# Seven products in place of eight for gate and value, their weights streamed from memory, and PReLU by two ScalarE passes throughout

## The chip, the cores and the metric

One core of a Trainium2 chip runs the whole kernel as one program. The metric is device time in microseconds (us). Its engines are TensorE (PE in the profile; PEld is its weight load), VectorE (DVE), ScalarE (ACT), GpSimd (POOL) and SyncE (SP), which issues all DMAs here. Each engine works through its own list of instructions in order. A scheduler has fixed those lists when the kernel was built, so that they can be read without running it.

## The reference

Three layers follow one another. The attention has 8 batches, 8 heads, 576 tokens and head size 64, and goes through 32 packed tokens; its output is a matrix `x` of 4608 tokens by 512. Then come two feed-forward layers:

```python
p_packed = sm_attn(p, k, v)
out = sm_attn(q, p_packed, p_packed)          # -> x, 4608 x 512
h = x @ w_in                                  # 512 x 2048
g = np.maximum(h, 0.0) + alpha * np.minimum(h, 0.0)
x = g @ w_out                                 # 2048 x 512
g = x @ w_gate                                # 512 x 1536
silu = g * (1.0 / (1.0 + np.exp(-g)))
val = x @ w_val                               # 512 x 1536
return silu * val @ w_out2                    # 1536 x 512
```

## The kernel before

Weights arrive as the bits of float64 numbers. `convert` turns a piece of 128 by 512 of them into float32 on the chip: one ScalarE, five VectorE and one GpSimd operation, and two more that split it into a high and a low part. A product of float32 accuracy is made of three TensorE passes over such parts (`mm3`, lines 281 to 283: low weight by high input, high by high, high by low).

**First layer.** An iteration (256 in all) takes 128 of the 2048 hidden numbers and 288 tokens. `h_unit` makes their hidden values `h` in a PSUM bank (tag `h`, two banks): six matmuls of 288 columns. PReLU follows, in iterations below `RELU` by two ScalarE rectifications and one VectorE operation (lines 699 to 701), from there on by two VectorE operations (lines 705 and 708). `split` then makes the high part on ScalarE (line 716) and the low part on GpSimd (line 718). `o_unit` multiplies them by `w_out` two iterations later (`LAG1`): 12 matmuls of 288 columns into the four banks `acc`. Beside these products run the attention of the next batch (`quad`), and `pp_win`, which multiplies its packed values by `w_in`.

**Second layer.** An iteration (108 in all) takes 128 hidden numbers and a block of `T` = 512 tokens. `gv_unit` makes `gps` (gate, tag `h`) and then `vps` (value, tag `at`), 12 matmuls of 512 columns each. ScalarE takes the sigmoid of `gps` (line 817), VectorE multiplies by `gps` and by `vps` (lines 818, 819), and `split` makes two parts. `out_unit` multiplies them by `w_out2` one iteration later (`LAG2`), 12 matmuls of 512 columns into `acc`. All weights of the layer lie in SBUF; their 36 pieces are converted by the table `PIECES2` in the last 40 iterations of the first layer and the first 6 of the second. The layer's input is read back from memory (`x1d`) and split block by block.

The order of the work around the change is set by tables of iterations (`plan`, `at`) and then by the scheduler, which moves instructions on each engine by what it expects to be ready.

Of the kernel before, what the change touches and what calls it, by code (L numbers as in the profile page):

```python
# [12 lines left out]
ALU = mybir.AluOpType  # L13
# [50 lines left out]
# The first layer's pieces in order: 128 columns of w_in, 128 rows of w_out.  # L64
# [10 lines left out]
# Later batches' attention: steps by iteration, for each group of four heads from its own start.  # L75
# [7 lines left out]
# Iterations from the second feed-forward's start: its weights' pieces, and load and split of its  # L83
# input, of the first block and of the next ones (from the start of the block before).
PIECES2 = {
    -40: 1, -35: 1, -32: 3, -31: 1, -24: 1, -23: 1, -7: 1, -3: 5, -2: 1, -1: 3, 1: 1, 2: 2, 4: 1,
    5: 3, 6: 7,
}
FIRST_X = ((-10, -8), (-6, -6), (-6, -4), (-1, -1))
NEXT_X = ((7, 11), (4, 5), (9, 9), (11, 11))  # L90

# High words of float64 numbers at the ends of float32's exponent range, as float32 bits.
# [9 lines left out]
def tile_kernel(  # L102
# [34 lines left out]
    NBLK = NT // T  # L137
# [25 lines left out]
    # ---- weights: float64 bits to float32, or to two float32r parts  # L163
    win, wout, wg, wv, wo2 = {}, {}, {}, {}, {}

    SLOTS = dict(wi="AABB", wo="AABB", wg="AAB", wv="BAB", wp="CCD")
# [37 lines left out]

    def convert(n=1):
        """The next n pieces of 128 by 512 numbers."""
        for src, parts in queue[:n]:
# [4 lines left out]
            issued.append(nc.sync.dma_start(out=like(raw, src), in_=src))  # L212
            words = raw.rearrange("p (n t) -> p n t", t=2)
            low, high = words[:, :, 0], words[:, :, 1]
            held = n_piece in HOLD
            with tc.issue_after(begun[HOLD[n_piece]].ins) if held else ExitStack():
                nc.scalar.activation(out=f32(val), in_=f32(high), func=AF.Abs)
            nc.vector.tensor_scalar(
                out=f32(val), in0=f32(val), scalar1=E_TOP, scalar2=E_LOW, op0=ALU.min, op1=ALU.max
            )  # L220
            nc.vector.tensor_scalar(
                out=val,
                in0=val,
                scalar1=3,
                scalar2=0x3FFFFFF8,
                op0=ALU.logical_shift_left,
                op1=ALU.bitwise_and,
            )
            nc.vector.scalar_tensor_tensor(
                out=val,  # L230
                in0=high,
                scalar=0xC0000000,
                in1=val,
                op0=ALU.bitwise_and,
                op1=ALU.bitwise_or,
            )
            nc.vector.tensor_scalar(
                out=high, in0=val, scalar1=0xFF800000, scalar2=None, op0=ALU.bitwise_and
            )
            dst = parts()  # L240
            light = len(dst) == 1
            if n_piece in BY_POOL:
                nc.scalar.activation(out=f32(low), in_=low, func=AF.Copy, scale=2.0**-52)
                nc.gpsimd.tensor_tensor(out=f32(low), in0=f32(low), in1=f32(high), op=ALU.mult)
            else:
                nc.vector.scalar_tensor_tensor(
                    out=f32(low),
                    in0=low,
                    scalar=2.0**-52,
                    in1=f32(high),  # L250
# [656 lines left out]
```

## Time and profile before

| | us |
|---|---|
| median of 3 runs | 1799.95 (1799.92 to 1800.79) |
| span of the profiled execution | 1797.2 |
| PE busy | 1712.5 (95% of the span) |
| DVE, ACT, POOL busy | 886.2, 534.1, 556.5 |
| first matmul of the second layer's gate | 883.55 |

The profile cuts the span into 40 slices; a digit is the busy share of a slice in tenths, and PEclk is the granted TensorE clock, in tenths of full speed:

```profile
PE   6698899999999999998788999999999999999999
DVE  7999965655656474778996312122121212121211
ACT  5765442323233332433332212111121212121111
POOL 3666622222222222366765211111111111111111
PEclk7899999999999999999999999999999999999999
```

The first five slices hold the attention of the first batches and the first layer's weights. Then the first layer runs; slices 17 to 22 hold the conversion of the second layer's weights, and the rest is the second layer.

### The profile page before, as it was taken

Reading aid. Unit: us, or ns where it says so; the run is one execution under the profiler, and the core shown is the slowest. Engines: PE = TensorE matmul, PEld = TensorE weight load, DVE = VectorE, ACT = ScalarE, POOL = GpSimd, SP = SyncE. Lnnn points to the kernel's source line nnn. Section 1 sums busy time; section 2 is a strip of 40 time slices with the busy share of each in tenths; the row PEclk is TensorE's granted clock in tenths of the full one; section 3 lists DMA queues with packets and bytes.
Section 4 is the critical chain, followed back from the end, with each engine's and each line's share of the span. In section 5 each row is a group of like instructions: output and inputs, shape, how many; then the busy total and the mean of one; then the engine's idle time right before and its main releaser. Section 6 shows DMA issues by size and latency. Waiting matters only on the chain.

```text
span 1797.2 us, 24797 instructions
## 1 busy us (share of the span) xinstructions
PE 1712.5 (95%) x9616; PEld 1433.5 (80%) x9616; DVE 886.2 (49%) x1509; ACT 534.1 (30%) x1125; POOL 556.5 (31%) x524
## 2 busy tenths in 40 slices
PE   6698899999999999998788999999999999999999
PEld 3477688888888888888666888888888888888887
DVE  7999965655656474778996312122121212121211
ACT  5765442323233332433332212111121212121111
POOL 3666622222222222366765211111111111111111
PEclk7899999999999999999999999999999999999999
DMA  9333451412222222113241101000010101010000
GB/s 241 109 103 122 132 129 42 81 27 55 43 52 53 55 53 42 61 40 107 93 132 50 56 1 47 1 30 18 1 47 1 47 1 47 1 36 1 24 0 24
DMA packets 179349, 99.13 MB, mean 55 GB/s; under 512 B 125984, under 2 KB 164896, under 8 KB 179232
## 3 DMA queue, kind: packets, MB, share of 16 engines
q1 hardware_dynamic: 179232, 97.56, 20.2%
q8 instruction: 75, 1.23, 0.3%
q14 instruction: 42, 0.34, 0.1%
HBM read 76.29 MB, written 21.23 MB: 54 GB/s over the span
## 4 chain that ended last, share of the span: by engine, by line
PE 78%; DVE 11%; issue 3%; ACT 2%; POOL 2%; DMA 2%; SPq 0%; POOLq 0%; DVEq 0%; ACTq 0%
PE acc L281 6%; PE acc L283 6%; PE acc L282 6%; PE o L281 5%; PE o L282 5%; PE vps L281 5%; PE vps L282 5%; PE o L283 5%; PE vps L283 5%; PE gps L283 5%; PE gps L282 5%; PE gps L281 5%; PE ppw L577 3%; PE h L281 3%; PE h L283 3%
## 5 line engine op out<-in xcount | busy, mean ns | idle before, releaser
L718 POOL TENSOR_TENSOR lo<-g,hi 128x288 fp32r<-128x288 f32 x256 | 220.8, 864 | 451.1 <-ACT hi L716 421.1
L718 POOL TENSOR_TENSOR lo<-s,hi 128x512 fp32r<-128x512 f32 x108 | 141.4, 1309 | 679.2 <-ACT hi L716 679.2
L818 DVE TENSOR_TENSOR s<-gps,s 128x512 f32<-128x512 f32 x108 | 74.6, 691 | 481.9 <-ACT s L817 481.9
L716 ACT ACTIVATE hi<-g 128x288 fp32r<-128x288 f32 x256 | 113.1, 443 | 357.8 <-DVE g L708 281.5
L705 DVE TENSOR_SCALAR g<-h,al 128x288 f32<-128x288 f32 x208 | 106.9, 514 | 171.6 <-PE h L283 154.1
L281 PE MATMUL h<-a2h,ppw 128*128 128x288 f32 x512 | 158.3, 309 | 18.2 <-DVE g L708 12.4
L817 ACT ACTIVATE s<-gps 128x512 f32<-128x512 f32 x108 | 64.4, 596 | 367.8 <-PE gps L283 367.8
L282 PE MATMUL h<-a2h,ppw 128*128 128x288 f32 x512 | 151.9, 297 | 0.0
L283 PE MATMUL h<-a2l,ppw 128*128 128x288 f32 x512 | 151.7, 297 | 0.0
L716 ACT ACTIVATE hi<-s 128x512 fp32r<-128x512 f32 x108 | 68.1, 631 | 254.8 <-DVE s L819 254.8
L819 DVE TENSOR_TENSOR s<-vps,s 128x512 f32<-128x512 f32 x108 | 74.5, 690 | 120.0 <-PE vps L283 119.8
L281 PEld LDWEIGHTS h<-a2h,ppw 128*128 128x128 f32 x512 | 96.7, 189 | 46.3 <-DVE g L708 18.3
L283 PEld LDWEIGHTS h<-a2l,ppw 128*128 128x128 f32 x512 | 96.3, 188 | 1.7 <-issue 1.7
L282 PEld LDWEIGHTS h<-a2h,ppw 128*128 128x128 f32 x512 | 96.9, 189 | 0.1
L708 DVE SCALAR_TENSOR_TENSOR g<-h,g 128x288 f32<-128x288 f32 x208 | 93.9, 453 | 4.4
L577 PE MATMUL ppw<-wi,ppT 128*64 128x512 f32 x256 | 78.0, 632 | 10.3 <-POOL wi L255 7.0
L281 PE MATMUL acc<-hi,wo0l 128*128 128x288 f32 x256 | 78.2, 310 | 4.5 <-ACT hi L716 3.7
L281 PE MATMUL acc<-hi,wo1l 128*128 128x288 f32 x256 | 74.8, 301 | 3.9 <-ACT hi L716 3.7
L282 PE MATMUL acc<-hi,wo0h 128*128 128x288 f32 x256 | 75.5, 300 | 0.0
L282 PE MATMUL acc<-hi,wo2h 128*128 128x288 f32 x256 | 75.3, 299 | 0.0
L281 PE MATMUL acc<-hi,wo2l 128*128 128x288 f32 x256 | 75.0, 299 | 0.1
L281 PE MATMUL acc<-hi,wo3l 128*128 128x288 f32 x256 | 74.6, 298 | 0.4 <-ACT hi L716 0.4
(224 smaller groups left out, 4556.8 us busy)
## 6 DMA issues: line engine op xcount, KB each, us to landing
cva<-in_moe_w_out_dram SPq DMA_DIRECT2D x24, 512.0 KB, 3.5
v<-in_v_dram SPq DMA_DIRECT2D x16, 576.0 KB, 4.8
out_dram<-os SPq DMA_DIRECT2D x36, 256.0 KB, 2.1
cva<-in_moe_w_in_dram SPq DMA_DIRECT2D x16, 512.0 KB, 3.6
kr<-in_k_dram SPq DMA_DIRECT2D x96, 72.0 KB, 2.7
qr<-in_q_dram SPq DMA_DIRECT2D x96, 72.0 KB, 2.4
x1d<-x1s SPq DMA_DIRECT2D x24, 288.0 KB, 2.1
cva<-in_moe_w_gate_dram SPq DMA_DIRECT2D x12, 512.0 KB, 3.7
```

The lines of the kernel that those rows point to most:

```text
L281: nc.tensor.matmul(o, wlo, xhi, start=start, stop=False)
L282: nc.tensor.matmul(o, whi, xhi, start=False, stop=False)
L283: nc.tensor.matmul(o, whi, xlo, start=False, stop=stop)
L577: nc.tensor.matmul(o[r, :], ppT[NQ * b + q2][:, r], w[:, 2 * q2 + pr, :], start=True, stop=True)
L705: nc.vector.tensor_scalar(out=g32, in0=hp, scalar1=0.0, scalar2=al[:, f : f + 1], op0=ALU.min, op1=ALU.mult)
L708: nc.vector.scalar_tensor_tensor(out=g32, in0=hp, scalar=0.0, in1=g32, op0=ALU.max, op1=ALU.add)
L716: nc.scalar.activation(out=hi, in_=x, func=AF.Copy)
L718: nc.gpsimd.tensor_tensor(out=lo, in0=x, in1=f32(hi), op=ALU.subtract)
L817: nc.scalar.activation(out=s, in_=pt["g"], func=AF.Sigmoid)
L818: nc.vector.tensor_tensor(out=s, in0=pt["g"], in1=s, op=ALU.mult)
L819: nc.vector.tensor_tensor(out=s, in0=pt["v"], in1=s, op=ALU.mult)
```

## The change

**Second layer, products.** Two blocks of 384 tokens (`T` = 384) form a super-block. Its input is cut into four parts by token block and by halves of the 512 inputs (A11, A12, A21, A22), and 128 columns of gate and of value into four likewise. Eight products of such parts would make gate and value for both blocks; seven products of sums and differences of parts do (Winograd's form of Strassen's scheme). `gv_step` runs one step, 72 in all: seven products of 6 matmuls of 384 columns, in three accumulations. `xb` (tag `h`) collects products 0 and 2, `yb` (tag `at`) products 1, 3 and 5, and `vb` (tag `h` again) products 4 and 6. The intermediate sums are read out of a bank in between, before the next product is added to it: `p1` by ScalarE, `u2`, `u3` and again `p1` by VectorE. Two blocks mean two results of 384 columns, one finished on VectorE (`s1`), the other on GpSimd (`s2`). `out_unit` takes 9 matmuls of 512 columns for each block; for block two it needs two more accumulators than `acc` has, and holds one bank of tag `h` and one of `at` for a whole super-block, so that `xb` and `vb` share one bank, and `yb` has one.

**Second layer, weights.** They are no longer resident. In 12 groups from iteration 44 on, one every 17 iterations in the table, `columns2` converts a gate and a value piece, `product2` makes the seven weight parts in two parts each and writes them to memory (`wgvd`), and `rows2` does so for `w_out2`. In the second layer `load_gv` reads 2 tiles of 128 by 1792 numbers for each step, two steps ahead, and `load_wo2` loads `w_out2` once.

**First layer.** `RELU` goes from 48 to 256: all iterations rectify on ScalarE.

```diff
-T = 512
+T = 384
-LAG2 = 1
-RELU = 48
+RELU = 256
-PIECES2 = {
-    -40: 1, -35: 1, -32: 3, -31: 1, -24: 1, -23: 1, -7: 1, -3: 5, -2: 1, -1: 3, 1: 1, 2: 2, 4: 1,
...
+GROUP0, GROUP_STEP = 44, 17
+GATE_AT, VAL_AT, PRODUCTS_AT, OUT_AT = 0, 4, (7, 8, 9, 10, 11, 12, 13), 14
+PRODUCTS = ("A11", "S2", "A12", "S3", "S1", "A22", "S4")
...
+    def product2(f, k):
...
+        if k == 0:
+            for out, x, y in ((t1, b12, b11), (t2, b22, t1), (t3, b22, b12), (t4, b21, t2)):
+                nc.gpsimd.tensor_tensor(out=out, in0=x, in1=y, op=ALU.subtract)
+        full = (b11, t2, b21, t3, t1, t4, b22)[k]
...
+        nc.scalar.activation(out=hi, in_=full, func=AF.Copy)
+        nc.gpsimd.tensor_tensor(out=lo, in0=full, in1=f32(hi), op=ALU.subtract)
+        nc.sync.dma_start(
+            out=wgvd[f][:, :, k, :], in_=f32(stage).rearrange("p (t n) -> p t n", t=2)
+        )
...
+    def load_gv(n):
...
+        gvw[n] = [
+            wpool.tile([P, 7, 2 * P], F32R, tag="C", name=f"gv{n}_{t}", bufs=WBUFS["C"])
+            for t in range(2)
+        ]
+        for t in range(2):
+            nc.sync.dma_start(out=f32(gvw[n][t]), in_=wgvd[f][:, t])
...
+        xb, yb = bank("h", "xb"), bank("at", "yb")
+        product(xb, n, 0, True)
+        nc.scalar.activation(out=p1, in_=xb, func=AF.Copy)
+        product(yb, n, 1, True)
+        add(u2, yb, p1)
+        product(xb, n, 2, False)
+        nc.scalar.activation(out=s1, in_=xb, func=AF.Sigmoid)
+        nc.vector.tensor_tensor(out=s1, in0=xb, in1=s1, op=ALU.mult)
+        product(yb, n, 3, False)
+        add(u3, yb, p1)
...
+        between(0)
+        xb = bank("h", "vb")
+        product(xb, n, 4, True)
+        add(u3, xb, u3)
...
+        product(yb, n, 5, False)
+        add(p1, yb, p1)
...
+        nc.scalar.activation(out=s2, in_=p1, func=AF.Sigmoid)
+        nc.gpsimd.tensor_tensor(out=s2, in0=s2, in1=p1, op=ALU.mult)
+        product(xb, n, 6, False)
+        add(u2, xb, u2)
+        nc.vector.tensor_tensor(out=s1, in0=s1, in1=u2, op=ALU.mult)
+        halves(n, 0, s1)
+        nc.gpsimd.tensor_tensor(out=s2, in0=s2, in1=u3, op=ALU.mult)
+        halves(n, 1, s2)
+        between(1)
...
+        load_gv(n + 2)
+    ACC = ("acc0", "acc1", "acc2"), ("acc3", "h", "at")
...
+        if f == NF2 - 1:
+            o = vp.tile([P, T // P, DM], F32, tag="v", name=f"os{s}_{t}")
```

`between(0)` and `between(1)` stand for the two `out_unit` of the step before. The new functions that convert and split are `widen` (the operations of `convert`, unchanged), `sums_x` and `split_x` (sums, differences and parts of the input).

On TensorE, the second layer before: the gate products of iteration 67 (`gps67`) begin behind the last output product (`o3`), and run without a break into one bank.

```order
L281 MATMUL o3_5_13174<-wp1h_10053,lo321_13352 128x512
L282 MATMUL o3_5_13174<-wp1h_10053,hi321_13350 128x512
L283 MATMUL o3_5_13174<-wp1l_10054,hi321_13350 128x512
L281 MATMUL gps67_13420<-x2h5_0_13050,wg1l_9745 128x512 [waits DVE_49]
L282 MATMUL gps67_13420<-x2h5_0_13050,wg1h_9744 128x512
L283 MATMUL gps67_13420<-x2l5_0_13051,wg1h_9744 128x512
L281 MATMUL gps67_13420<-x2h5_1_12754,wg1l_9745 128x512
```

The same engine now, in step 27: the first matmuls of each product of the step, in their order (`gv27` are the streamed weights, `o00` and `o10` the output products of step 26).

```order
L287 MATMUL yb27_13506<-xS2_2_13120,gv27_1_13405 128x384 [waits DMAHW1_49,DVE_49]
L288 MATMUL yb27_13506<-xS2_2_13120,gv27_0_13404 128x384 [waits DMAHW0_49]
...
L287 MATMUL xb27_13505<-xA11_2_12888,gv27_1_13405 128x384 [waits DVE_49]
...
L287 MATMUL xb27_13505<-xA12_2_13142,gv27_1_13405 128x384 [waits Activation_49]
...
L287 MATMUL yb27_13506<-xS3_2_13154,gv27_1_13405 128x384 [waits DVE_49]
...
L287 MATMUL o00_2_13346<-wp1_10427,pl26_0_13480 128x512 [waits Pool_49]
...
L287 MATMUL o10_2_13392<-wp1_10427,pl26_1_13485 128x512 [waits Pool_49]
...
L287 MATMUL vb27_13545<-xS1_2_13187,gv27_1_13405 128x384 [waits DVE_49]
...
L287 MATMUL yb27_13506<-xA22_2_13192,gv27_1_13405 128x384 [waits DVE_49]
...
L287 MATMUL vb27_13545<-xS4_2_13199,gv27_1_13405 128x384 [waits DVE_49]
```

The scheduler has put product 1 (`yb27`, input S2) ahead of product 0 (`xb27`, input A11), so that product 2 (input A12) follows product 0 at once, into the same bank, and waits for ScalarE. 64 of the 72 steps have this order.

On ScalarE, the first layer around iteration 150 before: one operation per iteration, and the attention's between them.

```order
L716 ACTIVATE hi149_6223<-g32_149_6220 128x288 [waits DVE_49,PE_49,Pool_49]
L526 ACTIVATE s2t_11_6188<-s2t_11_6188 128x576 [waits DMAHW4_49,DMAHW3_49,DMAHW5_49,DMAHW2_49,DVE_49]
L716 ACTIVATE hi150_6249<-g32_150_6246 128x288 [waits DVE_49,PE_49,Pool_49]
L716 ACTIVATE hi151_6275<-g32_151_6272 128x288 [waits DVE_49,PE_49,Pool_49]
L580 ACTIVATE ppw5_2_6291<-ppw5_20_6292 128x512 [waits PE_49]
```

The same place now (`L699` makes the high part of a streamed weight):

```order
L753 ACTIVATE r_150_6801<-h150_6793 128x288 [waits PE_49,Activation_49]
L754 ACTIVATE g32_150_6800<-h150_6793 128x288 [waits Pool_49]
L770 ACTIVATE hi150_6805<-g32_150_6800 128x288 [waits DVE_49]
L532 ACTIVATE s2t_11_6740<-s2t_11_6740 128x576 [waits DVE_49]
L753 ACTIVATE r_151_6837<-h151_6829 128x288 [waits PE_49,Activation_49]
L754 ACTIVATE g32_151_6836<-h151_6829 128x288 [waits Pool_49]
L586 ACTIVATE ppw5_2_6857<-ppw5_20_6858 128x512 [waits PE_49]
L699 ACTIVATE cva1_103<-cva1_103 128x256 [waits DMAHW0_49,Pool_49]
L770 ACTIVATE hi151_6841<-g32_151_6836 128x288 [waits DVE_49]
```

Three operations per iteration now stand in a row: the two rectifications free the bank `h`, and the next iteration's stand behind the high part, which waits for VectorE.

## Rows read from the trace of the kernel before

**Rows 1.** The page: the span and its instructions.

```profile
span 1797.2 us, 24797 instructions
```

**Rows 2.** Busy time of each engine by stretch (PEclk is the granted clock).

```profile
core 0: us, PE busy (x) PEld busy (x) DVE busy (x) ACT busy (x) POOL busy (x), PEclk, DMA share, GB/s
100.00:150.00 50.00, 45.38 (x323) 38.65 (x322) 46.47 (x72) 29.96 (x76) 32.24 (x29) 1.00 0.42 111
300.00:350.00 50.00, 50.00 (x379) 44.72 (x377) 26.65 (x59) 15.64 (x42) 12.86 (x16) 1.00 0.24 50
800.00:850.00 50.00, 44.06 (x308) 41.56 (x309) 43.66 (x73) 19.14 (x38) 32.95 (x29) 1.00 0.36 115
850.00:900.00 50.00, 36.87 (x236) 33.58 (x235) 47.02 (x66) 16.74 (x32) 39.06 (x31) 0.96 0.27 87
900.00:950.00 50.00, 43.85 (x173) 35.11 (x173) 49.41 (x59) 17.49 (x30) 32.28 (x23) 0.91 0.41 125
950.00:1000.00 50.00, 42.81 (x183) 33.78 (x182) 30.85 (x40) 14.00 (x24) 26.47 (x20) 1.00 0.12 43
```

**Rows 3.** What PE waited for, 740 to 1010 us: total, times, longest.

```profile
PE o L281 <- POOL lo L718: 13.3, 7, 3.8
PE h L281 <- DVE g L708: 12.4, 9, 2.7
PE gps L281 <- DVE s L818: 7.0, 1, 7.0
```

**Rows 4.** Timeline, second layer: start, us, instruction, [idle before <- releaser].

```profile
1300.21 0.39 PE L281 MATMUL gps<-x2h,wg0l 128*128 128x512 f32 x1
...
1301.34 0.39 PE L283 MATMUL gps<-x2l,wg0h 128*128 128x512 f32 x1
...
1301.83 0.60 ACT L817 ACTIVATE s<-gps 128x512 f32<-128x512 f32 x1 [4.17 <-PE gps L283]
...
1304.29 0.39 PE L281 MATMUL o<-wp2h,lo 128*128 128x512 f32 x1
...
1306.81 0.39 PE L283 MATMUL o<-wp2l,hi 128*128 128x512 f32 x1
```

**Rows 5.** Timeline, first layer: 12 output matmuls of one iteration, first and last.

```profile
612.15 0.30 PE L281 MATMUL acc<-hi,wo1l 128*128 128x288 f32 x1
...
613.60 0.29 PE L283 MATMUL acc<-lo,wo1h 128*128 128x288 f32 x1
```

**Rows 6.** Timeline around a wait of PE for VectorE.

```profile
814.44 0.45 DVE L708 SCALAR_TENSOR_TENSOR g<-h,g 128x288 f32<-128x288 f32 x1
...
814.94 0.40 PE L281 MATMUL h<-a2h,ppw 128*128 128x288 f32 x1 [2.35 <-DVE g L708]
...
815.17 0.30 PE L282 MATMUL h<-a2h,ppw 128*128 128x288 f32 x1
```

**Rows 7.** Page, groups: busy, mean ns of one, idle before and its releaser.

```profile
L718 POOL TENSOR_TENSOR lo<-g,hi 128x288 fp32r<-128x288 f32 x256 | 220.8, 864 | 451.1 <-ACT hi L716 421.1
L718 POOL TENSOR_TENSOR lo<-s,hi 128x512 fp32r<-128x512 f32 x108 | 141.4, 1309 | 679.2 <-ACT hi L716 679.2
L818 DVE TENSOR_TENSOR s<-gps,s 128x512 f32<-128x512 f32 x108 | 74.6, 691 | 481.9 <-ACT s L817 481.9
...
L705 DVE TENSOR_SCALAR g<-h,al 128x288 f32<-128x288 f32 x208 | 106.9, 514 | 171.6 <-PE h L283 154.1
...
L708 DVE SCALAR_TENSOR_TENSOR g<-h,g 128x288 f32<-128x288 f32 x208 | 93.9, 453 | 4.4
```

**Rows 8.** Groups by form: two of VectorE, then one of ScalarE (up to 1000 us).

```profile
L229 DVE SCALAR_TENSOR_TENSOR cvb<-cva,cvb 128x512 uint32<-128x512 uint32 x35 | 38.2, 1091 | 0.4
...
L701 DVE SCALAR_TENSOR_TENSOR g<-g,nal,r 128x288 f32<-128x288 f32 x48 | 36.1, 752 | 11.0 <-ACT g L700 11.0
...
L744 ACT ACTIVATE x1s<-acc 128x288 f32<-128x288 f32 x32 | 12.9, 410 | 18.7 <-PE acc L283 18.1
```

**Rows 9.** DMA issues: engine, count, KB each, median us from issue to landing.

```profile
cva<-in_moe_w_gate_dram SPq DMA_DIRECT2D x12, 512.0 KB, 3.7
...
xr<-x1d SPq DMA_DIRECT2D x8, 16.0 KB, 1.9
```

More of the change, by code (lines that the diff above doesn't have):

```diff
@@ L203, in use, with widen @@
         vals[:] = sum((v for _, v in cut), [])
+    def widen(src, raw, val, out=None, n_piece=-1):
+        issued.append(nc.sync.dma_start(out=like(raw, src), in_=src))
+        words = raw.rearrange("p (n t) -> p n t", t=2)
+        low, high = words[:, :, 0], words[:, :, 1]
+        held = n_piece in HOLD
+        with tc.issue_after(begun[HOLD[n_piece]].ins) if held else ExitStack():
+            nc.scalar.activation(out=f32(val), in_=f32(high), func=AF.Abs)
+        nc.vector.tensor_scalar(
+            out=f32(val), in0=f32(val), scalar1=E_TOP, scalar2=E_LOW, op0=ALU.min, op1=ALU.max
+        )
+        nc.vector.tensor_scalar(
+            out=val,
+            in0=val,
+            scalar1=3,
+            scalar2=0x3FFFFFF8,
+            op0=ALU.logical_shift_left,
+            op1=ALU.bitwise_and,
+        )
+        nc.vector.scalar_tensor_tensor(
+            out=val,
+            in0=high,
+            scalar=0xC0000000,
+            in1=val,
+            op0=ALU.bitwise_and,
+            op1=ALU.bitwise_or,
+        )
+        nc.vector.tensor_scalar(
+            out=high, in0=val, scalar1=0xFF800000, scalar2=None, op0=ALU.bitwise_and
+        )
+        if n_piece in BY_POOL:
+            nc.scalar.activation(out=f32(low), in_=low, func=AF.Copy, scale=2.0**-52)
+            nc.gpsimd.tensor_tensor(out=f32(low), in0=f32(low), in1=f32(high), op=ALU.mult)
+        else:
+            nc.vector.scalar_tensor_tensor(
+                out=f32(low),
+                in0=low,
+                scalar=2.0**-52,
+                in1=f32(high),
+                op0=ALU.mult,
+                op1=ALU.mult,
+            )
+        full = f32(val) if out is None else like(f32(val), out)
+        other = f32(low) if out is None else like(f32(low), out)
+        nc.gpsimd.tensor_tensor(
+            out=full if out is None else out, in0=full, in1=other, op=ALU.add
+        )
     def convert(n=1):
@@ L211, in convert @@
             n_piece = len(issued)
[L212 to L239, printed above, removed]
             dst = parts()
             light = len(dst) == 1
[L242 to L250, printed above, removed]
-                    op0=ALU.mult,
-                    op1=ALU.mult,
-                )
-            full = like(f32(val), dst[0])
-            nc.gpsimd.tensor_tensor(
-                out=dst[0] if light else full, in0=full, in1=like(f32(low), dst[0]), op=ALU.add
-            )
+            widen(src, raw, val, dst[0] if light else None, n_piece)
             if not light:
                 hi, lo = dst
+                full = like(f32(val), hi)
                 nc.scalar.activation(out=hi, in_=full, func=AF.Copy)
@@ L650, in tile_kernel @@
         at(*key, lambda script=script: run(script))
-    at(NB1, 0, lambda: use(*space))
     for b in range(2, B):
@@ new lines, in tile_kernel, with product @@
+    for n in ("load", "A11", "S", "S2", "A22", "A12", "S4", "S3", "S1"):
+        fn = dict(load=lambda: load_x(0), S=lambda: sums_x(0)).get(
+            n, lambda n=n: split_x(0, n)
+        )
+        at(N1 + FIRST_X[n], 1, fn)
+    at(N1 - 9, 0, table)
+    at(N1 - 8, 0, lambda: load_gv(0))
+    at(N1 - 1, 0, lambda: load_gv(1))
+    for i in range(2):
+        at(N1 - 12, 0, lambda i=i: load_wo2(i))
+    for i in range(2, NF2 // 2):
+        at(N1, 1, lambda i=i: load_wo2(i))
+    def product(bank, n, k, start):
+        s = n // NF2
+        x = xs2[s, PRODUCTS[k]]
+        hi, lo = gvw[n]
+        for e in range(2):
+            c = slice(e * P, (e + 1) * P)
+            mm3(
+                bank,
+                (hi[:, k, c], lo[:, k, c]),
+                (x[:, 0, e], x[:, 1, e]),
+                start and e == 0,
+                e == 1,
+                skip_group_check=True,
+            )
@@ L776, in tile_kernel @@
-    for i in range(NBLK):
-        for cc in range(KC):
-            load, cut = (NEXT_X if i else FIRST_X)[cc]
-            it = N1 + NF2 * max(i - 1, 0)
-            at(it + load, 0, lambda i=i, cc=cc: load_x(i, cc))
-            at(it + cut, 1, lambda i=i, cc=cc: split_x(i, cc))
-    def weights2():
-        use(*space, cut_up(vscratch("cvb1"), 0))
-        queue.extend(
-            cols(w_gate, wg, "wg", 0)
-            + cols(w_val, wv, "wv", 0)
-            + rows(w_out2, wo2, "wp", 0)
-            + cols(w_gate, wg, "wg", 1)
-            + cols(w_val, wv, "wv", 1)
-            + rows(w_out2, wo2, "wp", 1)
-            + cols(w_gate, wg, "wg", 2)
-            + cols(w_val, wv, "wv", 2)
-        )
@@ L860, in tile_kernel @@
     gp2 = ctx.enter_context(tc.tile_pool(name="g2", bufs=1))
[L861 to L869 removed]
+    for n in range(NBLK * NF2):
+        gv_step(n, lambda t, n=n: out_unit(n - 1, t) if n else None)
+    for t in range(2):
+        out_unit(NBLK * NF2 - 1, t)
 _INS = [
```

249 lines of the change are left out of this document (157 added, 92 removed).

## The prediction, made before the changed kernel ran

> **What bounds the kernel now.** I read the busy time by stretch first. In the first layer's middle (300 to 350 us) PE is busy for the whole 50 us while ScalarE works 15.6, and in the second layer's steady part only the timeline is left to read: matmuls of 512 columns begin every (1301.34 − 1300.21)/5 = 0.2265 us for the gate and every (1306.81 − 1304.29)/11 = 0.229 us for the output [rows 2, 4]. PE is the bound, except at 800 to 1000 us, where the second layer's weights are converted and VectorE is busy up to 49.4 of 50 us [rows 2]. The list of waits there shows PE behind the low part of POOL, PReLU on VectorE, and once 7.0 us behind the product with the sigmoid [rows 3]. So the change can gain by fewer columns on PE, and at that place; it can lose wherever PE has to wait anew.
>
> **Products of the second layer.** Before: 108 × 24 = 2592 gate and value matmuls × 0.2265 = 587.1 us. After: 72 × 42 = 3024 of 384 columns. The trace has none of that width. The bounds are the two neighbours: 288 columns take (613.60 − 612.15)/11 = 0.132 [rows 5] and 512 take 0.2265. Between them the time goes with the columns, 0.132 + 96/224 × 0.0945 = 0.1725, and 3024 × 0.1725 = 521.6 us. **−65.5 us.** Output matmuls stay at 1296 of 512 columns (108 × 12, 72 × 18): 0.
>
> **The wait inside a step.** In 64 of 72 steps product 2 stands right behind product 0 on PE, into the same bank, and ScalarE has to copy the bank out in between (the order of step 27 above). Nothing of the step that could run meanwhile stands between them, and PE is in order, so the whole hand-over is uncovered; behind it every product of the step, the output products and so the next step are late by it. Its parts, none of which this kernel shows for 384 columns: the last matmul's end lies past its share of pace, 0.39 − 0.227 = 0.16, and ScalarE starts 0.10 behind the end (1301.34 + 0.39 = 1301.73 to 1301.83) [rows 4]; the copy takes between 0.41 (288 columns) and 0.60 (512), so 0.41 + 0.43 × 0.19 = 0.49 [rows 4, 8]; PE starts 814.94 − (814.44 + 0.45) = 0.05 behind its releaser, and the second matmul after such a wait starts 0.23 behind the first in place of 0.132, so 0.10 more [rows 6]. Sum 0.90 us per step, 64 × 0.90 = **+57.6 us**. Bounds: the ScalarE operation and handing over alone, about 0.6 (38 us); with 512 columns' price and a second slow start, 1.1 (70 us).
>
> The other banks have cover. A step on PE is 42 × 0.1725 + 18 × 0.229 = 11.37 us, 12.27 with the wait, and 18 output matmuls (4.1 us) stand between products 3 and 4, so that VectorE's reads of `yb` and the sigmoid fall beside them. Narrower are product 6 behind the read of product 4, with product 5 (1.04 us) as cover, and the next step's first product behind the last read of `yb`, covered by product 6. A VectorE read of 384 columns costs between 0.453 (288) and 0.691 (512) [rows 7], 0.55 by columns; with 0.16 + 0.10 + 0.05 around it 0.86, which leaves 0.2 us. I cost them at nothing; without that cover see rival three.
>
> **The layer change.** Piecewise conversion at 800 to 1000 us goes. PE's idle time there was 5.94 + 13.13 + 6.15 + 7.19 = 32.4 us; the granted clock of 0.96 and 0.91 cost 0.04 × 36.87 + 0.09 × 43.85 = 5.4; and 17 waits of the three kinds listed ended late by the modelled end and start, 17 × 0.26 = 4.4 [rows 2, 3]. **−42 us**, of which between −25 and −42 may come, since part of the idle time could belong to attention's last work. New there: step 1's 1.8 MB of weights stand on SP's queue behind the output weights, **+3** (0 to 8).
>
> **Layer one.** Conversions and products of weights now lie beside iterations of the middle, a group about every 41 us. Each `cvb`-like operation of VectorE costs 1.09 us for 512 columns [rows 8]; one group adds at most 3 × 5 × 1.09 = 16 us to VectorE per 41 us, and VectorE's PReLU falls from 0.514 + 0.453 to 0.752 at most per iteration [rows 7, 8]. Over 50 us with 26.65 us of VectorE work, there is space [rows 2]. ScalarE gets 2 × 0.41 and loses nothing: three operations per iteration, and the next one's rectifications queue behind the high part, which waits for VectorE. Serial, that is 0.41 + 0.41 + 0.752 + 0.41, about 2.0 us with hand-overs against 18 × 0.132 = 2.38 on PE, so it fits, narrowly. Lower end 0 by the row at 300 us, upper end the stretch at 100 us, where VectorE has 46.47 of 50 and PE stands idle 4.6: 490 us of conversion × 4.6/50 = 45 [rows 2]. I take the value near the first row, **+8**.
>
> The Trainium skill, "SBUF — State Buffer", section "SBUF: two separate sides", says that a VectorE operation with two inputs in SBUF and a GpSimd operation that reads SBUF exclude each other for their whole length. The changed PReLU line has two such inputs where the old one read PSUM, and its row agrees in direction: 752 ns against 453 [rows 7, 8]. By the rule the 0.752 can grow by a POOL operation's rest (0.86 at most [rows 7]), to 1.6, and an iteration on ScalarE to 2.9 us, over PE's 2.38; that is in rival four.
>
> **Stream and edges.** A load of 512 KB takes 3.7 us and one of 16 KB 1.9, so 0.508 MB per 1.8 us, 282 GB/s; 1.835 MB then land in 1.9 + 6.5 = 8.4 us, inside a step of 12.27 [rows 9]. Issued two steps ahead: 0. At each of five inner super-block edges 0.79 MB come in and go out, and ScalarE and VectorE form sums and parts beside the step: **+7.5** (5 × 1.5; 0 to 15). At the end the last step's chain is bare: two VectorE operations 2 × 0.555, the high part 0.49, the low part 0.864 + 0.43 × 0.445 = 1.055 [rows 7], with starts 3.0; the last output is 0.52 MB larger, 1.9. **+4.9** (2 to 7).
>
> **Sum.** −65.5 + 57.6 − 42 + 3 + 8 + 7.5 + 4.9 = −26.5. The profiled span of 1797.2 [rows 1] becomes 1770.7; the median lies 2.75 above that span (1799.95), so **1773 us**.
>
> **Rivals.**
> One: the wait is hidden, because ScalarE reads the bank while the last passes run or the pace does not break. For it: nothing in rows 6; every wait there costs. Then 1773 − 57 = 1716.
> Two, on the other side: the stream is late. With input, output and weights a step moves about 1.835 + 0.13 + 0.13 = 2.10 MB, 171 GB/s over 12.27 us. If the fixed part of a load doesn't overlap, the rate is 0.524/3.7 = 142 GB/s [rows 9], a step takes 14.8 us, and 72 × 2.5 = 182 us are added: 1955. It decides from below 171 GB/s. The highest stretch has 125 GB/s at a DMA share of 0.41, which speaks for over 300 at a full share, and against this rival [rows 2].
> Three: the hand-overs with 0.2 us of margin come late too, since VectorE has two of them behind one another and `s1` between. 0.4 us × 2 × 72 = 58: 1831.
> Four: the first layer is bound by ScalarE and VectorE. 0.2 us in 150 of the 256 iterations makes 30: 1803; from 0.18 us per iteration on it eats the whole gain. For it: 2.0 against 2.38 is narrow, and attention's exponentials use ScalarE too (15.64 of 50 us [rows 2]); against it: products wait for `g` only two iterations later.
> Five: PE's clock, whose levels are 1.2 and 2.4 GHz (1.00 in the rows). Stretches with idle PE were granted 0.91 and 0.96, yet one with 7.19 us idle had 1.00 [rows 2], so short waits alone don't lower it. If one per step did, at 0.91 over about 880 us of second layer: + 80, 1853.
> On this the Trainium skill, "TensorE: Matmul & The Clock Gate", section "A second HAM failure mode: psum-queue depth-cycling", says that frequent short idle times between groups of matmuls made the clock swing between its two levels. Rows 2 show both outcomes, so it gets a small chance.
>
> **How the numbers follow.** Forecast 0.68, with 1755 to 1793 its own range (the wait's 38 to 70, layer one's 0 to 25, the layer change's 25 to 42). Rival one 0.07, two 0.05, three 0.06, four 0.12, five 0.02. About 0.2% (3.6 us) is what a measurement of this kernel can tell from no change. Faster: 0.68 + 0.07 + 0.05 of rival four = 0.80; the same: 0.03 of it; slower: 0.04 of it and 0.13 of two, three and five = 0.17. The range for 8 in 10 takes in rival four's centre on one side and the best edge on the other: 1745 to 1804.
>
> **What would show it.** 384-column matmuls every 0.172 us; in 64 steps one idle time of PE before product 2, ended by the ScalarE copy, with matmul starts about 0.9 us further apart than the pace; steps of 12.3 us; no PE idle of many us at 850 to 1000; the second layer beginning some 40 us earlier less layer one's loss. Wrong would be: waits for DMA queues before `yb` (rival two), waits for VectorE before products 1 and 6 (three), waits for `g` or for bank `h` spread over iterations 47 to 197 (four), a granted clock below 1.00 in the second layer (five).

## The result and the profile after

| kernel | median of 4 runs, us | ratio to before, 95% interval |
|---|---|---|
| before, beside it | 1800.37 (1799.92 to 1802.49) | |
| changed | 1816.5 (1814.24 to 1826.16) | 1.0095 [1.0076, 1.0114] |

The changed kernel is 0.95% slower; 1773 us was forecast, with a range of 1745 to 1804. The profiled execution is the slowest of the four (1826.16 us), so that the terms below are compared in its own span: 1824.4 against 1797.2 [rows 1], 27.2 us more, where the sum said 26.5 less.

First the page of the changed kernel: the span, the busy times, and the slices of PE and its clock.

```profile
span 1824.4 us, 27304 instructions
...
PE 1694.5 (93%) x10048; PEld 1478.5 (81%) x10048; DVE 996.9 (55%) x1667; ACT 734.3 (40%) x1800; POOL 805.8 (44%) x824
...
PE   5698899999999999999999999999998999999997
...
PEclk8799999999999999999999999999998999999999
```

TensorE is busy for 18 us less (1712.5 before) and the kernel takes 27 us more. The stretches that answer to [rows 2], and two of the second layer:

```profile
core 0: us, PE busy (x) PEld busy (x) DVE busy (x) ACT busy (x) POOL busy (x), PEclk, DMA share, GB/s
...
300.00:350.00 50.00, 48.05 (x343) 41.20 (x342) 31.71 (x55) 27.84 (x81) 28.31 (x32) 1.00 0.53 144
...
850.00:900.00 50.00, 48.18 (x354) 47.54 (x354) 22.16 (x39) 26.33 (x68) 17.87 (x20) 1.00 0.49 163
900.00:950.00 50.00, 48.52 (x251) 44.22 (x250) 17.76 (x30) 10.32 (x21) 16.49 (x16) 1.00 0.53 190
...
1100.00:1150.00 50.00, 47.67 (x245) 43.29 (x244) 17.20 (x28) 9.63 (x20) 16.59 (x16) 1.00 0.41 148
...
1350.00:1400.00 50.00, 44.80 (x207) 39.53 (x206) 20.35 (x33) 11.50 (x23) 17.74 (x17) 0.90 0.52 187
```

The layer change went as hoped: at 850 to 950 us PE is busy for 96.7 of 100 us, where it was busy for 80.7, and its clock stays at the upper level. Two stretches are worse than foreseen. In layer one, at 300 us, 343 matmuls stand where there were 379. And at 1350 us, where one super-block follows another, 207 stand against 245 in a steady stretch, at a lower mean clock.

What PE waited for in the changed kernel (us in total, times, longest), which answers to [rows 3]:

```profile
PE xb L287 <- ACT p L928: 39.9, 64, 2.0
PE acc L287 <- ACT hi L770: 11.9, 17, 1.6
PE xb L287 <- DVE u L911: 8.7, 4, 2.2
...
PE yb L287 <- DMA gv<-wgvd: 1.5, 1, 1.5
```

The first line is the wait foreseen, 64 times. The streamed weights were late once, by 1.5 us.

The hand-over inside a step, in the timeline (start, us, instruction, idle time before it and its releaser):

```profile
1311.69 0.34 PE L289 MATMUL xb<-xA,gv 128*128 128x384 f32 x1
1312.09 0.47 ACT L928 ACTIVATE p<-xb 128x384 f32<-128x384 f32 x1
...
1312.61 0.45 PE L287 MATMUL xb<-xA,gv 128*128 128x384 f32 x1 [0.58 <-ACT p L928]
1312.89 0.34 PE L288 MATMUL xb<-xA,gv 128*128 128x384 f32 x1
```

From the last matmul of product 0 to the first of product 2 it is 0.92 us where the pace is 0.173; the list shows only 0.58 of it as idle, since the matmul's modelled end hides the rest. The second matmul follows after 0.28. A step takes 1312.61 − 1300.32 = 12.29 us, against 42 × 0.1733 + 18 × 0.229 = 11.40 without the wait: 0.89 us per step.

| term | forecast, us | in the profile, us |
|---|---|---|
| products (3024 × 0.1733 against 587.1) | −65.5 | −63.0 |
| wait in a step (64 × 0.89) | +57.6 | +57.0 |
| layer one, iterations 48 to 224 (536.2 to 567.5) | +8 | +31.3 |
| five super-block edges, over steady steps | +7.5 | +31.7 |
| the end: from the last gate or value matmul to the end of the span, without the output matmuls (4.4 to 12.7) | +4.9 | +8.3 |
| all else: layer change and first steps, by difference | −39 | −38 |

At the end PE waits 3.5 us for the last low part, 3.3 us more pass behind the last matmul (7.5 for 4.2), and the clock falls once more.

An iteration is timed from its first `h` matmul in the trace; an edge from the first output matmul of a steady step to that of a steady step five later, as here from 1172.77 to 1240.78, 68.0 us where 5 × 12.29 = 61.5 (the five edges: 6.7, 6.6, 8.6, 6.7 and, over four steps, 3.2). In the profiles of `relu48`, `hi_pool` and `pin` below, which have the same second layer, the five edges cost 26 to 27 us by the same reading, so some of the 31.7 belongs to this one execution.

```profile
1172.77 0.39 PE L287 MATMUL o<-wp,pl 128*128 128x512 f32 x1
...
1240.78 0.39 PE L287 MATMUL o<-wp,pl 128*128 128x512 f32 x1
```

VectorE, GpSimd and PE at the same edge:

```profile
1216.49 1.03 DVE L832 TENSOR_TENSOR xs<-xr,xr 128x384 f32<-128x384 f32 x2 [3.35 <-DMA out_dram<-os]
...
1217.13 2.23 POOL L833 TENSOR_TENSOR xr<-xr,xr 128x384 f32<-128x384 f32 x2 [5.26 <-DVE xs L832]
...
1218.42 2.62 DVE L840 TENSOR_TENSOR xr<-xs,xr 128x384 f32<-128x384 f32 x2 [0.44 <-POOL xr L833]
...
1219.32 1.30 POOL L949 TENSOR_TENSOR s<-s,p 128x384 f32<-128x384 f32 x1
...
1220.96 0.55 DVE L911 TENSOR_TENSOR u<-vb,u 128x384 f32<-128x384 f32 x1
...
1221.56 0.44 PE L287 MATMUL xb<-xA,gv 128*128 128x384 f32 x1 [2.20 <-DVE u L911]
...
1222.22 0.53 PE L287 MATMUL xb<-xA,gv 128*128 128x384 f32 x1
...
1222.55 0.53 PE L288 MATMUL xb<-xA,gv 128*128 128x384 f32 x1
...
1223.97 0.69 PE L287 MATMUL xb<-xA,gv 128*128 128x384 f32 x1 [0.58 <-ACT p L928]
```

The sums of a later super-block's input (L832, L840) wait for an output transfer and for POOL, and VectorE's last read of the bank (L911) is queued behind them: PE stands for 2.2 us. Most of that is the length of the two L840. The line shows them together; in the trace they take 1.35 and 1.34 us. Each begins while a GpSimd operation runs (the second L833, then L949) and ends 0.42 us behind that operation's end. It is so for all eight L840 between 1000 and 1600 us, 1.34 to 1.36 us each; in the run `edges` below no GpSimd operation runs beside them, and all ten take 0.55. By that, some 1.6 of the 2.2 us come from working beside GpSimd. After the stop PE's clock falls (columns as above):

```profile
1211.00:1224.00 13.00, 10.22 (x49) 8.46 (x47) 6.98 (x11) 2.11 (x5) 6.55 (x6) 0.93 0.72 252
1224.00:1237.00 13.00, 13.00 (x56) 11.88 (x57) 3.74 (x7) 1.34 (x3) 1.83 (x2) 0.81 0.06 10
```

From 1222.22 on matmuls start 0.32 us apart, where the pace is 0.173: the clock fell some 0.6 us after PE had resumed, ahead of its next wait (0.58 us, to 1223.97). By the mean clock in windows around the five edges (0.72 to 0.81 over 8 to 18 us) the lower level cost 3.4, 3.4, 5.0, 3.4 and 1.7 us, an estimate of about 17 of the 31.7 us.

### The profile page after: what moved, and what is told of

Its sections match the earlier page's. It is cut to its first block, busy times and chain, and to the rows that moved or that the text cites. A ratio compares the mean times of both kernels' runs of the same rounds, so it can differ in the third digit from the quotient of the medians.

```text
span 1824.4 us, 27304 instructions
## 1 busy us (share of the span) xinstructions
PE 1694.5 (93%) x10048; PEld 1478.5 (81%) x10048; DVE 996.9 (55%) x1667; ACT 734.3 (40%) x1800; POOL 805.8 (44%) x824
## 4 chain that ended last, share of the span: by engine, by line
PE 56%; DVE 16%; DMA 7%; issue 7%; ACT 6%; POOL 6%; SPq 1%; POOLq 0%; ACTq 0%; DVEq 0%
PE o L288 5%; PE o L289 5%; PE o L287 5%; PE acc L287 4%; PE acc L289 4%; PE acc L288 3%; DVE s L952 3%; PE yb L287 3%; PE yb L288 3%; PE yb L289 3%; PE vb L287 2%; PE vb L289 2%; PE vb L288 2%; PE xb L287 2%; DVE u L911 2%
## 5 line engine op out<-in xcount | busy, mean ns | idle before, releaser
L949 POOL TENSOR_TENSOR s<-s,p 128x384 f32<-128x384 f32 x72 | 75.2, 1045 | 563.9 <-ACT s L948 563.9
L755 DVE SCALAR_TENSOR_TENSOR g<-g,nal,r 128x288 f32<-128x288 f32 x256 | 173.4, 677 | 176.0 <-ACT g L754 174.3
L911 DVE TENSOR_TENSOR u<-vb,u 128x384 f32<-128x384 f32 x144 | 80.2, 557 | 296.1 <-PE vb L289 295.9
L287 PE MATMUL o<-wp,pl 128*128 128x512 f32 x432 | 171.6, 397 | 3.5 <-POOL pl L975 3.5
L289 PE MATMUL o<-wp,ph 128*128 128x512 f32 x432 | 172.4, 399 | 0.0
L288 PE MATMUL o<-wp,ph 128*128 128x512 f32 x432 | 172.4, 399 | 0.0
L287 PE MATMUL xb<-xA,gv 128*128 128x384 f32 x288 | 107.2, 372 | 48.8 <-ACT p L928 39.9
L975 POOL TENSOR_TENSOR pl<-s,ph 128x384 fp32r<-128x384 f32 x144 | 144.3, 1019 | 15.9 <-ACT ph L973 14.3
L911 DVE TENSOR_TENSOR u<-yb,p 128x384 f32<-128x384 f32 x144 | 79.5, 552 | 81.6 <-ACT p L928 66.3
L287 PEld LDWEIGHTS h<-a2h,ppw 128*128 128x128 f32 x512 | 97.0, 189 | 30.4 <-ACT g L754 9.4
L753 ACT ACTIVATE r<-h 128x288 f32<-128x288 f32 x256 | 102.1, 399 | 32.3 <-PE h L289 31.7
L287 PE MATMUL yb<-xS,gv 128*128 128x384 f32 x288 | 98.2, 341 | 6.8 <-DVE u L911 4.4
L754 ACT ACTIVATE g<-h 128x288 f32<-128x288 f32 x256 | 103.8, 405 | 0.6 <-POOL lo L772 0.6
L289 PE MATMUL xb<-xA,gv 128*128 128x384 f32 x288 | 99.6, 346 | 0.0
```

Of the source, the lines that this page charges most:

```text
L287: nc.tensor.matmul(o, wlo, xhi, start=start, stop=False, **kw)
L288: nc.tensor.matmul(o, whi, xhi, start=False, stop=False, **kw)
L289: nc.tensor.matmul(o, whi, xlo, start=False, stop=stop, **kw)
L753: begun[it] = nc.scalar.activation(out=r, in_=hp, func=AF.Relu)
L754: nc.scalar.activation(out=g32, in_=hp, func=AF.Relu, scale=-1.0)
L755: nc.vector.scalar_tensor_tensor(out=g32, in0=g32, scalar=nal[:, f : f + 1], in1=r, op0=ALU.mult, op1=ALU.add)
```

## The experiments

Two terms were far off, layer one and the edges, and the wait was as computed. The experiments ask whether the wait is what it seems, what the edges cost, and what in layer one costs 31 us: PReLU on ScalarE (theory A, rival four), the conversions' work (theory B), or ScalarE standing in line behind conversion operations that wait for transfers (theory C, formed from the list below). "Iterations 48 to 208" is the part of layer one in which the kernel before converts nothing. Each ratio is to the kernel before measured beside that run. How finely the last column can be read: `changed`, `cover`, `edges` and `cover_edges` have the same first layer and lie between 513.3 and 515.7, `pin` and `best` have the same too and lie 4.6 apart.

| kernel | median, us | ratio to before, 95% interval | iterations 48 to 208, us |
|---|---|---|---|
| before | | | 486.9 |
| changed | 1816.5 | 1.0095 [1.0076, 1.0114] | 515.7 |
| relu48 | 1809.27 | 1.0045 [1.0028, 1.0061] | 505.5 |
| before_relu256 | 1814.43 | 1.0065 [1.005, 1.008] | 489.1 |
| cover | 1745.42 | 0.9686 [0.9672, 0.9701] | 513.3 |
| edges | 1801.92 | 1.0002 [0.9992, 1.0011] | 514.5 |
| pin | 1809.83 | 1.0052 [1.0037, 1.0067] | 503.4 |
| cover_edges | 1760.28 | 0.9772 [0.9755, 0.9788] | 514.1 |
| best (cover, edges, pin) | 1751.84 | 0.9732 [0.9709, 0.9754] | 498.8 |
| best_relu48 | 1738.71 | 0.9667 [0.9647, 0.9686] | 492.8 |
| hi_pool | 1805.08 | 1.0021 [1.0008, 1.0035] | 497.6 |
| cover_pin_relu48 | 1726.52 | 0.9583 [0.9569, 0.9597] | 493.6 |
| cover_pin_alt | 1729.74 | 0.9603 [0.9588, 0.9617] | 497.0 |
| cover_pin_hipool | 1723.97 | 0.9572 [0.9555, 0.959] | 489.5 |

### PReLU alone and conversions alone

```diff
-RELU = 256
+RELU = 48
```

> The changed kernel, but PReLU by two VectorE operations from iteration 48 on, as before the change; the conversions stay spread over layer one, and the second layer is the changed one. Iterations 48 to 224 took 536.2 us before and 567.4 us with the change. Theory A, ScalarE's chain of two rectifications and the high part makes the loss (rival four): they take 536 to 545 us and the whole about 1790 us (1816.5 - 27). Theory B, the conversions between the iterations make it, whichever engine does PReLU: 560 us or more, the whole 1809 to 1825 us.

The reverse edit in the kernel before:

```diff
-RELU = 48
+RELU = 256
```

> The kernel before, with PReLU by two ScalarE rectifications and one VectorE operation in all iterations; nothing else changed. Theory A: iterations 48 to 224 take 555 us or more in place of 536.2, and the whole about 1820 us. Theory B: they take 534 to 541 us; the whole lies between 1785 us (VectorE relieved by 0.3 us per iteration where the weights are converted) and 1805 us.

Neither theory came out (iterations 48 to 224: 554.8 us in `relu48`, 548.0 in `before_relu256`). In iterations 48 to 208 PReLU on ScalarE without conversions costs 2.2 us (486.9 to 489.1), no more than the spread just named, conversions with PReLU on VectorE 18.6 (505.5), both 28.8 (515.7), 8 more than their sum. And the kernel before with ScalarE's PReLU lost 12.5 us (1814.43 against 1801.88); in its profile 4.6 of the loss are in iterations 208 to 248, where its conversions lie, but 4.3 stand ahead of iteration 48 and 4.2 in the second layer, where the edit changes nothing by itself. So PReLU on ScalarE costs little by itself, and, as far as this shows, more beside conversions. ScalarE's list of waits at 245 to 745 us in the changed kernel shows what they share (us in total, times, longest). The first line has its like in the kernel before; waits of conversions, as in the other three, the kernel before has none there:

```profile
ACT hi L770 <- DVE g L755: 109.1, 104, 3.7
ACT cva L699 <- DMA wgvd<-cva: 24.2, 22, 4.0
ACT cva L212 <- DMA cva<-in_moe_w_val_dram: 16.3, 9, 3.3
ACT cva L212 <- POOL cva L710: 7.2, 6, 2.4
```

And one such place in ScalarE's timeline:

```profile
401.10 0.44 ACT L770 ACTIVATE hi<-g 128x288 fp32r<-128x288 f32 x1 [0.99 <-DVE g L755]
...
405.94 0.67 ACT L212 ACTIVATE cva<-cva 128x512 f32<-128x512 f32 x1 [3.27 <-DMA cva<-in_moe_w_val_dram]
...
409.24 0.44 ACT L770 ACTIVATE hi<-g 128x288 fp32r<-128x288 f32 x1 [0.66 <-DVE g L755]
```

The scheduler put an operation that needs a load (L212) ahead of the rectifications; ScalarE waits 3.27 us for the load, and 8 us lie between two high parts, where an iteration takes 3. This shows ScalarE late, not yet PE: PE's list has no wait at 400 to 412 us, as it went on with other products meanwhile. Whether layer one's loss comes from such places only an edit can tell.

### Conversions held in place, and taken off ScalarE

The loads go ahead, and ScalarE's operations may not be moved ahead of their iteration:

```diff
-GROUP0, GROUP_STEP = 44, 17
+GROUP0, GROUP_STEP = 40, 17
+LOADS_AT = (0, 5, 12)
...
-        nc.scalar.activation(out=hi, in_=full, func=AF.Copy)
+        with tc.issue_after(begun[it].ins):
+            nc.scalar.activation(out=hi, in_=full, func=AF.Copy)
```

> The changed kernel, but the conversions in layer one are held in place: their loads go out two iterations or more ahead, and ScalarE's operations on them stand behind the first rectification of the iteration that the table names (groups every 17 iterations, from 40 on), where the scheduler had moved them ahead, so that ScalarE stood waiting for their transfers (24.2 + 16.3 + 6.9 + 6.7 us in iterations 48 to 224) with the rectifications and high parts behind. The same operations remain. Theory C, ScalarE held by transfers makes most of layer one's loss: iterations 48 to 224 take at most 552 us in place of 567.5 (536.2 before the change), the whole about 1800 us. Rival, the amount of work on VectorE, ScalarE and GpSimd makes it: 560 us or more and 1809 us or more.

Iterations 48 to 224 take 556.3 us, between the two bounds, and the whole 1809.83, on the rival's side. The edit only thinned the waits out (the line for L699 is still 24.3 us), and as its groups end later, fewer conversions are left in iterations 48 to 208 (139 VectorE operations of theirs, where the changed kernel has 170). So it could not decide. The next edit takes 96 of the waiting operations off ScalarE:

```diff
-        nc.scalar.activation(out=hi, in_=full, func=AF.Copy)
+        nc.gpsimd.tensor_copy(out=hi, in_=full)
...
-        nc.scalar.activation(out=stage[0], in_=f32(val), func=AF.Copy)
+        nc.gpsimd.tensor_copy(out=stage[0], in_=f32(val))
```

> The changed kernel, but the high part of each converted weight (7 products and one row piece for each of 12 groups, 96 operations that wait for a transfer or for GpSimd) is made by GpSimd in place of ScalarE, so that ScalarE's rectifications and high parts of layer one never stand behind them. Theory C, ScalarE held by waiting operations: iterations 48 to 208 take at most 505 us in place of 515.7 (486.9 before the change), the whole 1806 us or less. Rival: GpSimd, which makes the low part of layer one's hidden values, is held in ScalarE's place: 512 us or more, and 1812 us or more.

As theory C expected: 497.6 us in place of 515.7, and 1805.08. From iteration 48 to the second layer's first matmul, where it doesn't count in which iterations the conversions lie, it is 616.6 us in place of 632.7 (`pin`: 625.0). GpSimd now waits for the same transfers, 38.8 us at 245 to 745 us, and PE's list of waits there has nothing for GpSimd; the reason may be that the low part which GpSimd makes is multiplied last. Two things stay open: 497.6 is still 10.7 above the kernel before, and the edit takes about 42 us of work off ScalarE as well as the waits (in iterations 48 to 208). That the waits count and not the work is argued from `pin`, where ScalarE is busy for the same 0.67 of that stretch as in the changed kernel. What ScalarE waits for now is its inputs:

```profile
ACT hi L770 <- DVE g L755: 129.0, 129, 3.1
ACT r L753 <- PE h L289: 38.0, 52, 2.3
```

Waiting for PE's `h` (L753) means that ScalarE is ahead of PE; in the changed kernel no such line was among the first ten at this place.

### Cover for the wait

The second block's output products lag two steps and stand between products 0 and 2:

```diff
-        product(xb, n, 0, True)
+        last = product(xb, n, 0, True)
...
-        product(xb, n, 2, False)
+        with tc.issue_after(last.ins):
+            last = between(1, 2) or last
+        with tc.issue_after(last.ins):
+            product(xb, n, 2, False)
...
-        product(yb, n, 3, False)
+        last = product(yb, n, 3, False)
...
-        between(0)
+        with tc.issue_after(last.ins):
+            between(0, 1)
...
-        between(1)
```

> The changed kernel, but the second block's output products lag two steps in place of one and stand between product 0 and product 2 (9 matmuls of 512 columns, 2.06 us), so that they cover ScalarE's copy of the bank. Theory: the uncovered hand-over costs 0.89 us per step and nothing else is late by then: steps of 11.4 us in place of 12.29, 64 to 70 of them, so 57 to 62 us less, about 1757 us. Rival: the next hand-overs (product 6 behind VectorE's read, product 0 behind the last read) have margins of 0.2 us only and come late once the step is shorter: steps of 11.8 to 12.1 us, 1785 us or more.

1745.42 us, 71 less than the changed kernel and 3.1% less than before: the wait theory, and more than it promised. The waits of PE at 930 to 1600 us are down to this, from 43 us:

```profile
PE xb L287 <- DVE u L912: 2.6, 4, 0.7
PE o L287 <- POOL pl L979: 0.2, 1, 0.2
```

A steady step takes 11.49 us, 0.80 less, or 57 over 71 steps; the hand-over is the same, but PE works on beside it (product 0's last matmul, the copy, product 2's first):

```profile
1149.31 0.33 PE L289 MATMUL xb<-xA,gv 128*128 128x384 f32 x1
1149.71 0.47 ACT L929 ACTIVATE p<-xb 128x384 f32<-128x384 f32 x1
...
1151.57 0.33 PE L287 MATMUL xb<-xA,gv 128*128 128x384 f32 x1
```

The rest is the edges: the five now cost 1.2 to 1.8 us each over steady steps, 7.3 together. With 2.06 us of output products behind product 0, VectorE catches up there, and the granted clock is 1.00 from 100 to 1700 us.

### The edges

```diff
-        add(u3, yb, p1)
+        done = add(u3, yb, p1)
         if more:
-            split_x(s + 1, "S2")
+            with tc.issue_after(done.ins):
+                split_x(s + 1, "S2")
```

The same holds `sums_x_after` behind `done` in step 8.

> The changed kernel, but VectorE's sums and differences of the next super-block's input are held back to behind the third read of yb in step 8 and step 11 of a super-block, in place of where the scheduler moved them (behind the output's transfer, ahead of VectorE's read in the first steps of the next super-block). The five edges cost 31.7 us over steady steps. Theory: about 4.5 us of each (a wait of 2.3 us and a slow clock behind it) come from this place: 18 to 22 us less, 1795 to 1799 us, and no granted clock under 1.00 in the second layer's middle. Rival: the edges' cost comes from the transfers and copies of the output: within 5 us of 1816.5.

1801.92 us, 14.6 less: short of the 18 to 22 expected, and well over the rival's 5. The first three edges cost 2.9 to 3.1 us each, and the waits of `xb` for VectorE (8.7 us, 4 times) are gone. In their place PE waits once per edge for ScalarE's copy of the bank, 1.5 to 2.0 us, since the copy stands behind ScalarE's high part of a product, which waits for VectorE. The clock still shows 0.97 in the edges' stretches, so that part of the expectation failed.

> Both edits to the second layer: the output products as cover for ScalarE's copy, and VectorE's sums held back at the super-block edges. If the edges' loss is VectorE's own work ahead of its reads, and the cover does not already hide it, 8 to 12 us come off the 1745.4 of the cover alone: 1734 to 1738 us. Rival: the longer cover hides it already: 1742 to 1748 us.

Neither: 1760.28 us, 15 more than the cover alone. Held back, the splits of one edge stand in one block on VectorE, and the reads of the banks wait among them (VectorE, then PE's waits at 1170 to 1215 us):

```profile
1165.54 1.02 DVE L840 TENSOR_TENSOR xr<-xs,xr 128x384 f32<-128x384 f32 x2
...
1171.37 0.55 DVE L857 TENSOR_TENSOR xS<-xs,xS 128x384 fp32r<-128x384 f32 x1
...
1173.24 0.56 DVE L912 TENSOR_TENSOR u<-vb,u 128x384 f32<-128x384 f32 x1
```

```profile
PE xb L287 <- DVE u L912: 1.6, 2, 1.0
PE yb L287 <- ACT xS L856: 1.1, 1, 1.1
```

An edge costs 3.8 to 5.4 us there against 1.2 to 1.8 with the cover alone. What helped without cover hurts with it. Our reading, not tested further: the cover already gave VectorE the time, and the hold takes the freedom to spread.

### Combinations

> Cover, edges and conversions held in place together. If the three are independent: 1745.4 - 10 (edges) - 16 (layer one) = about 1720 us. Rival: conversions that end later (iteration 243 in place of 197) run into the preparation of the second layer's input and give it back at the layer change: 1730 us or more.

1751.84 us: missed, since the edges' edit cost what it cost above. The rival's bound is met, but not its mechanism: the second layer begins at 861.4 us, 17 earlier than in `cover_edges`.

> The same three edits, with PReLU by two VectorE operations from iteration 48 on. Theory C: with ScalarE no longer held by transfers the three ScalarE operations per iteration cost nothing, so this is the same as with them, within 4 us, or slower, since VectorE has 0.3 us more per iteration. Theory A (the chain itself): 7 us or more faster, as it was (1809.3 against 1816.5) without the three edits.

13 us faster than with PReLU on ScalarE: theory A's side, as long as ScalarE is still held by transfers (32.3 us in the line for L699 with this kernel).

> Cover, conversions held in place, and PReLU by two VectorE operations from iteration 48 on, without the edit of the edges, which cost 15 us beside the cover (1760.3 against 1745.4). If edges cost what cover shows (steps of 11.5 with one of 11.9 and one of 12.6 per edge, in place of one of 14.3 to 15.9): 5 x 2.5 to 4 us under the 1738.7 with all edits, about 1722 us. Rival: the edges' loss belongs to the state of layer one and the order that the scheduler makes of it: 1735 us or more.

1726.52 us, near the 1722 expected.

> The same, but from iteration 48 on PReLU goes by ScalarE in every odd iteration and by VectorE in every even one. If ScalarE's chain costs by each iteration that stands behind a conversion's operation, this lies half way between all on ScalarE and all on VectorE: layer one 3 us longer than with VectorE alone. If the loss comes from the more loaded of the two engines, it is shorter than either: 2 to 5 us less than the kernel with VectorE alone.

Slower by 3.4 us in iterations 48 to 208 (497.0 against 493.6) and by 3.2 in all. It leans to the first reading, but the two intervals overlap, so it does not decide.

> Cover, conversions held in place, high parts of converted weights on GpSimd, and PReLU on ScalarE in all iterations as in the changed kernel. If layer one's loss is ScalarE held behind waiting operations and nothing else, PReLU on ScalarE costs next to nothing here: iterations 48 to 208 take 490 to 495 us (493.6 with cover, conversions held and PReLU on VectorE; 489.1 for PReLU on ScalarE without conversions), the whole 1722 to 1730 us. Rival, the chain of three ScalarE operations costs by itself beside conversions: 498 us or more, 1731 us or more.

1723.97 us, 4.3% faster than before and the lowest of all, though not clear of `cover_pin_relu48`. Iterations 48 to 208 take 489.5 us, as PReLU on ScalarE takes without any conversion (489.1); `best`, with the high parts on ScalarE, takes 498.8. With conversions beside it, PReLU on ScalarE is as good as free once ScalarE hardly stands behind their transfers. The page of that kernel:

```profile
span 1720.6 us, 27265 instructions
...
PE 1653.6 (96%) x10048; PEld 1472.1 (86%) x10048; DVE 1008.7 (59%) x1667; ACT 709.1 (41%) x1704; POOL 850.4 (49%) x920
```

## Why the prediction was wrong

**What held.** The products, by a pace interpolated at 0.1725 and measured at 0.1733. The wait, term by term: forecast 0.90 us, measured 0.89, and confirmed by covering it. The stream, hidden: a median of 6.2 us to land for each of 144 loads, one wait of 1.5 us; rival two is out. The 0.2 us margins held in the steady steps; rival three is out there, but it is what happens at the edges. Rival one is out, since the wait costs its full size.

**Layer one, the step that failed first.** The step costed the conversions by busy time ("there is space") and took +8 where 31.3 came. It counted how many microseconds each engine works per iteration, and put ScalarE's rectifications behind the high part alone, not behind the conversions' own waits in the same queue. ScalarE was busy for only 27.84 of 50 us at 300 us, and late all the same: an operation that waits 1 to 4 us for a transfer holds the rectifications behind it, although its own work is 0.42 us. With 96 of these operations on GpSimd 18 of the 29 us came back, so ScalarE's queue is the place; that the waits in it count, and not the work, is argued, and the other 11 us stay open. Rival four named the right place, iterations 47 to 197, and the wrong mechanism: a chain of 2.0 us against 2.38 did fit, as 489.1 us without conversions shows. In PE's list only some 12 of the 29 us at 245 to 745 us appear as waits. The rest does not show as idle time, and no run separates it into causes. Is it that PE changes more often from one product to another? It does, 522 times against 473 in iterations 48 to 208, but hi_pool changes 525 times and is 18 us faster, so that is not the cause.

On the rule cited from the Trainium skill, "SBUF — State Buffer", section "SBUF: two separate sides", that a VectorE operation with two inputs in SBUF and a GpSimd operation that reads SBUF exclude each other for their whole length: the trace agrees with it, at the edges (L840 above) and in PReLU's VectorE operation.

```profile
L755 DVE SCALAR_TENSOR_TENSOR g<-g,nal,r 128x288 f32<-128x288 f32 x256 | 173.4, 677 | 176.0 <-ACT g L754 174.3
```

Of these 256, 142 began while a GpSimd operation was running. They took 806 ns on average and up to 1.57 us, and 112 of them ended 0.31 to 0.33 us behind that operation; the other 114 took 517 ns. The 0.752 of the prediction was such a mixture already: in the kernel before 25 take 0.51 us and 23 take 1.02. But layer one's loss does not come from this alone: in iterations 48 to 208 the mean is 677 ns in the changed kernel and 689 in `hi_pool`, which is 18 us faster.

**The edges, the second.** "5 × 1.5" was put at +7.5 with 15 as its upper end, as extra work beside the step; 31.7 came. The step did not ask where VectorE's sums would stand in its queue. They went ahead of the last read of a bank whose margin was 0.2 us, behind an output transfer and beside GpSimd, which made two of them 0.8 us longer each; PE stood 2.2 us for it, and the lower clock behind such stops made about 17 of the 31.7 us. Holding the sums back took 14.6 us off the whole; with the hand-over covered the edges cost 24 us less in the profile, and the clock did not fall.

**The clock.** Rival five came true at the edges alone. In steady steps, with one wait of 0.9 us each, the granted clock stays at the level of 2.4 GHz (1.00 at 1100 us). Behind a stop of 2.2 us the mean over 13 us fell to 0.81, which means that PE spent part of them at 1.2 GHz. The Trainium skill, "TensorE: Matmul & The Clock Gate", section "A second HAM failure mode: psum-queue depth-cycling", tells of frequent short idle times between groups of matmuls that make the clock swing. The waits of these steady steps did not, with 1.00 in that row.

**The rest.** From iteration 224 to the second layer's first matmul it is 65.2 us where it was 103.1, 38 less, inside the layer change's bounds. The end took 8.3 for 4.9.

With both failed terms at their measured size the sum is −26.5 + 23.3 + 24.2 = +21.0 for the profile's 27.2; the other 6.2 are the end (+3.4), the products (+2.5), all else (+0.9) and the wait (−0.6), by the rounded figures of the table.

## What to carry to other kernels

An engine's free time says nothing of whether background work can be put there: look at what each of its operations waits for, since an in-order queue hands that wait to whatever is behind it, and try operations that wait for transfers on an engine that the bottleneck does not wait for. Where one bank is read out between two products, put independent matmuls between them by an explicit order; the scheduler did not, and 2.06 us of output products as cover were worth 71 us. An edit that gains alone can lose beside another (the edges): try it again on the kernel that it is to stay in.

## What was not expected of the hardware

PE's idle times in the profile understate its waits: 0.58 us shown where matmul starts were 0.92 apart against a pace of 0.173. After a stop of 2.2 us the clock fell, some 0.6 us after PE had resumed, while 0.58 shown per 12.3 us, step after step, left it at 1.00. A VectorE operation whose inputs both lie in SBUF took 0.55 us with GpSimd idle and 1.35 when a GpSimd operation was already running (L840, 128x384). The changed kernel's four runs of the same program spread over 0.66% (1814.24 to 1826.16), the kernel before over 0.14%; what makes the difference is open, apart from the edges, which cost 26 to 31.7 us in four profiles with the same second layer.
